# First-stage spectra of a long convolution: stored in 128-row transfers, with 64 low and 26 high frequencies

## Chip, cores and metric

One core of one Trainium2 chip runs the whole program. The metric is the device time of one execution in microseconds (us), as the median of several runs.

## What is computed

A long causal convolution of each of eight sequences with one filter `h`, followed by a mixture of experts with soft slots. Cut to what matters:

```python
# x: (8, 5696, 128), h: (5696, 128)
Xf = rfft(x, n=2*S, axis=1); Hf = rfft(h, n=2*S, axis=0)
y  = irfft(Xf * Hf, n=2*S, axis=1)[:, :S, :]          # (8, 5696, 128)
x  = y.reshape(45568, 128)
logits = x @ phi                                       # 32 slots
d  = softmax over all rows of logits
slot_input = d.T @ x                                   # 32 x 128
slot_out   = relu(slot_input[e] @ w1[e]) @ w2[e]       # 8 experts, 4 slots each
c  = softmax over the slots of logits
out = c @ slot_out                                     # (45568, 128)
```

Everything is float32. The change touches the first stage of the Fourier transform of `h` and of the eight sequences.

## The kernel before

**The transform.** A sequence of 5696 = 89 x 64 positions is read as 89 rows of 64 positions, `n2` = 0..63, each with 128 channels. The first stage (`stage_a`, L230) is a matrix product over the rows that gives 90 frequencies `k1`, with a real and an imaginary part, for every `n2`. The second stage (`stage_b1`, L275) is, for each of the 90 frequencies, a matrix product over the 64 values of `n2`, after which the spectrum is multiplied with that of `h`. `stage_b2` goes back over `n2`, and the stages `c1` to `c6` go back over the rows, form the logits, both softmaxes and the sum over rows. The experts and the output product follow at the end.

**Between the stages the data go through DRAM.** Nine tensors `fd[g]` (g = 0 for `h`, 1 to 8 for the sequences) hold the spectra of the first stage as frequency x `n2` x (real, imaginary) x 128 channels. One value of `n2` is 1 KB, one frequency is a row of 64 KB. `stage_a` writes with short stretches of `n2` for many frequencies; `load_g` (L264) reads 8 frequencies with all 64 `n2` into the tile `gt`, 512 KB at a time, where the 128 partitions are 2 frequencies x 64 `n2`. Likewise `stage_b2` writes its result to the tensors `zm` and `zr`, and `load_main` and `load_rest` read them back into `zc` and `zx`.

**A chunk.** `load_x` brings 89 rows (96 for the sequences, cut at multiples of 16) of 2 x 8 values of `n2`. `fold` (L209, on POOL) adds and subtracts the near and the far positions. A chunk has 4 sums and 4 differences, that is 8 values of `n2`; the sums have the `n2` numbers 0 to 31 and the differences 32 to 63. Eight chunks make one `g`, 72 chunks all of them. The sums (o = 0) and differences (o = 1) go through different columns of the matrix `s1`.

**Low and high.** For each chunk `stage_a(c, False)` computes the low frequencies: two groups (o = 0 and 1) of 64 columns of `s1`, side by side in the 128 output partitions. For each pair of chunks `stage_a(c, True)` computes the high frequencies: four groups (two chunks, o = 0 and 1) of 32 columns. Each call makes two matrix products' worth of PSUM bank (real and imaginary part) and ACT copies both into one tile `fst` of 128 partitions x 4 KB, of which there are four buffers (L233, L243). With LOW = 60, 60 of each 64 low columns and 30 of each 32 high columns hold a frequency.

**Stores.** The stores of `fst` are not issued at once but put on the list `pending` (L221), which `flush` (L223) empties; the line of the issue in the profile is therefore L225. There are two stores of 60 rows for a low tile and four of 30 rows for a high one; a row is 4 KB, 4 values of `n2`. That makes 8 stores for a pair of chunks and 288 in all.

**Order.** The order of the work is written out by hand in the loop over steps `t` from L631. Chunk `t` is computed in step `t`; the second stage follows 9 steps behind (`LAG_B`) with one or two units of 8 frequencies in a step, the back transform 27 steps behind (`LAG_C`). Nearly all DMAs are issued by SP in program order: the loads of `x`, the stores `f<-fst`, the loads `gt<-f` (three buffers, requested three units ahead by `prefetch`, L638), the stores `zm<-zst` and `zr<-zst`, and the loads of `zc` and `zx`. The first load `gt` of a `g` waits until all stores of that `g` have landed. ACT's queue issues only the small constants and eight early stores `zr<-zx` of 24 rows. The very last DMA of the program (L901) writes the last 64 positions of all eight sequences:

```python
nc.sync.dma_start(
    out=ov[:, NV * RW * N2:, :].rearrange("b (j n) d -> b j (n d)", n=CH),
    in_=o_[:, n, :, :].rearrange("p q d -> p (q d)"))
```

Its target runs over 8 sequences and, within each, over 16 rows of 2 KB; its source is one tile of 128 partitions.

Of the kernel before, what the change touches and what calls it, by code (L numbers as in the profile page):

```python
# [11 lines left out]
F32 = mybir.dt.float32  # L12
# [6 lines left out]
def transform_tables(S, N1, N2, CH, LOW, MAIN, XR):  # L19

    N, R1, HALF, P = N1 * N2, S // N2, N2 // 2, 2 * N2
    k1 = np.arange(N1)  # L30
    alpha = np.pi * (k1 + 0.5) / N1
    m1 = np.arange(R1) - (N1 - 1) / 2
    a1 = np.outer(m1, alpha)
    part = np.stack([np.cos(a1), -np.sin(a1), -np.cos(a1)], 1)
    s1 = np.zeros((P, 2, 3, N2 + HALF))
    for i, r in enumerate((slice(0, R1), slice(XR - R1, XR))):
        s1[r, i, :, 0:LOW] = part[:, :, 0:LOW]
        s1[r, i, :, N2:N2 + N1 - LOW] = part[:, :, LOW:]
    a0 = np.outer(alpha, np.arange(N1 // 2) + 0.5)
    part = np.stack([np.cos(a0), -np.sin(a0), -np.cos(a0)], 1)  # L40
    NP = N1 // 2
    im = np.zeros((2, MAIN, 2, N2))
    ir = np.zeros((2, 2, HALF, N2))
    for o in range(2):
        for c in range(2):
            im[o, :, c, 0:NP] = part[0:MAIN, o + c]
            ir[o, c, 0:N1 - MAIN, 0:NP] = part[MAIN:, o + c]
    k2 = np.arange(N2)
    omega = np.pi * (k1[:, None] + 2 * N1 * k2[None] + 0.5) / N
    m2 = np.arange(HALF) - (N2 - 1) / 2  # L50
    a2 = m2[None, :, None] * omega[:, None, :]
    w = np.concatenate([np.cos(a2), np.sin(a2)], 1)
    back = np.arange(N2).reshape(2, HALF).T.reshape(-1)
    NU = (NP + 1) // 2
    turn = (N1 - 1) / 2 * alpha[:, None] + (N2 - 1) / 2 * omega
    wq = np.zeros((2, N2, NP, N2))
    vq = np.zeros((2, N2, NU, 2, N2))
    tn = np.zeros((2, N2, 2, (NU + 1) // 2, 2, 2))
    for a in range(2):
        wq[a] = w[a::2].transpose(1, 0, 2)  # L60
        for q in range(NP):
            vq[q % 2, :, q // 2, a] = w[2 * q + a][back].T
            tn[q % 2, :, 0, q // 4, a, q // 2 % 2] = np.cos(turn[2 * q + a]) / N
            tn[q % 2, :, 1, q // 4, a, q // 2 % 2] = np.sin(turn[2 * q + a]) / N
    im, ir, wq, vq, tn = [t.reshape(P, *t.shape[k:]) for t, k in
                          ((im, 2), (ir, 3), (wq, 2), (vq, 2), (tn, 2))]
    return [np.ascontiguousarray(t, dtype=np.float32) for t in (s1, im, ir, wq, vq, tn)]
# [3 lines left out]
def kernel(  # L71
# [24 lines left out]
    nc = tc.nc  # L96
    P = 128
    B, S, D = x.shape
    NSL = moe_phi.shape[1]
    E, _, F = moe_w1.shape  # L100
    SPE = NSL // E
    NFC = F // P
    N1, N2 = 90, 64
    R1, HALF, NP = S // N2, N2 // 2, N1 // 2
    CH = 4
    NJ = HALF // CH
# [5 lines left out]
    HP = P // 2  # L112
    NQ = NJ // 2
    assert S == R1 * N2 and R1 == N1 - 1 and D == P and CH == Q == 4
    LOW, MAIN = 60, HP
    XR = -(-R1 // 16) * 16
    ctx.enter_context(tc.manual_schedule())

# [1 line left out]
        nc.inline_tensor(t, f"tab_{n}").ap()  # L120
        for n, t in zip(("s1", "im", "ir", "w", "v", "turn"),
                        transform_tables(S, N1, N2, CH, LOW, MAIN, XR))]
    fd = [nc.dram_tensor(f"f_{g}", (N1, N2, 2, D), F32, kind="Internal").ap() for g in range(B + 1)]
    zm = [nc.dram_tensor(f"zm_{b}", (2, MAIN, HALF, 2, D), F32, kind="Internal").ap() for b in range(B)]
    zr = [nc.dram_tensor(f"zr_{b}", (2, 2, HALF, HALF, D), F32, kind="Internal").ap() for b in range(2)]
    cd = nc.dram_tensor("c_t", (P, B * NQ, Q, 2, MH), F32, kind="Internal").ap()
# [24 lines left out]
    front = ExitStack()  # L151
# [15 lines left out]
    def bank():  # L167
        rings.append(rings.pop(0))
        return rings[-1].tile([P, 512], F32, name="bank", tag="bank")
# [51 lines left out]
    pending = []  # L221
# [5 lines left out]
    def columns(c, o):  # L227
        return folded[c][:, o, :, :].rearrange("p n d -> p (n d)")

    def stage_a(c, high):  # L230

        g, j = divmod(c, NJ)
        st = apool.tile([P, CH, 2, D], F32, name="fst", tag="fst", bufs=4)  # L233
        if high:
            groups = [(c_, o, HALF, slice(HP, HP + HALF)) for c_ in (c - 1, c) for o in range(2)]
        else:
            groups = [(c, o, HP, slice(0, HP)) for o in range(2)]
        for q in range(2):
            p = bank()
            for i, (c_, o, m, cols) in enumerate(groups):  # L240
                nc.tensor.matmul(p[i * m:(i + 1) * m, :], s1[:, g // B, q + o, cols], columns(c_, o),  # L241
                                 start=True, stop=True)
            nc.scalar.activation(st[:, :, q, :],  # L243
                                 p[:, :].rearrange("p (n d) -> p n d", d=D), AF.Copy)
        k0, k1 = (LOW, N1) if high else (0, LOW)
        for i, (c_, o, m, _) in enumerate(groups):
            n0 = o * HALF + CH * (c_ % NJ)
            pending.append(partial(
                nc.sync.dma_start,
                out=fd[g][k0:k1, n0:n0 + CH, :, :].rearrange("k n c d -> k (n c d)"),  # L250
                in_=st[i * m:i * m + k1 - k0, :, :, :].rearrange("k n c d -> k (n c d)")))
        if high:
            for c_ in (c - 1, c):
                del folded[c_]
# [369 lines left out]
    for i in range(8):  # L624
        nc.scalar.dma_start(
            out=zr[i // 4][i // 2 % 2, i % 2, N1 - MAIN:].rearrange("k (j r) d -> (k j) (r d)", r=2 * CH),
            in_=zring[0][1][0:4 * (HALF - N1 + MAIN), :, :, :].rearrange("p h n d -> p (h n d)"))
# [3 lines left out]
    for t in range(last_front + 1):  # L631
# [24 lines left out]
        if t < NA:  # L656
            stage_a(t, False)
            fold(t + 1)
# [16 lines left out]
        if t % 2:  # L675
# [10 lines left out]
            if t < NA:  # L686
                stage_a(t, True)
# [54 lines left out]
    for q in range(Q):  # L742
        r = slice(q * NSL, (q + 1) * NSL)
        nc.gpsimd.tensor_copy(out=rep4[r, :, :],
                              in_=ident[r, r].unsqueeze(1).broadcast_to([NSL, Q, NSL]))
# [17 lines left out]
    for V in range(T, NT):  # L763
# [30 lines left out]
        else:  # L794
            for i in range(4 * (V - T - 1), min(4 * (V - T), E), 2):
                nc.sync.dma_start(
                    out=w2s[:, i:i + 2, :, :],
                    in_=moe_w2[i:i + 2].rearrange("e (p c) d -> p e c d", p=P))
# [6 lines left out]
    p = bank()  # L805
# [8 lines left out]
    p = bank()  # L814
# [5 lines left out]
                  ap=[own.ap[0], [NSL + SPE, E], [1, SPE]])  # L820
# [6 lines left out]
    for g in range(EG):  # L827
        for f0 in range(0, F, FH):
            p = bank()
# [3 lines left out]
            dst = hid[:, g, :, f0 // NFC:(f0 + FH) // NFC]  # L833
# [6 lines left out]
    for g in range(EG):  # L840
        for k0 in range(0, NFC, 4):
            p = bank()
            for k in range(4):
# [3 lines left out]
                out=hidT[:, g, k0:k0 + 4, :], in_=p[:, :].rearrange("p (k c) -> p k c", k=4))  # L847
# [9 lines left out]
    p = bank()  # L857
# [18 lines left out]
    for b in range(B):  # L876
        for w0 in range(0, NV, G4):
            n = min(G4, NV - w0)
# [10 lines left out]
            for q in range(Q):  # L889
                dst = o_[:, 0:n + lone, q, :]  # L890
# [7 lines left out]
                out=ov[b, t0:t0 + n * RW * N2, :].rearrange("(w p n) d -> p w (n d)", p=P, n=CH),  # L898
                in_=o_[:, 0:n, :, :].rearrange("p w q d -> p w (q d)"))
            if lone:  # L900
# [3 lines that stand above are left out]
# [29 lines left out]
```

## Time and profile before

| | |
|---|---|
| runs (us) | 909.78, 910.25, 915.08; median 910.25 |
| the profiled execution (us) | 909.23 |
| its span on the core (us) | 907.4 |
| PE busy | 760.2 us (84%) |
| DVE, ACT, POOL busy | 66%, 48%, 44% |
| bytes by DMA | 278.33 MB: HBM read 147.94 MB, written 129.00 MB |
| stores `f<-fst` | 144 of 240 KB and 144 of 120 KB, issued from 15.2 to 656.2 us |
| loads `gt<-f` | 99 of 512 KB and 9 of 128 KB, issued from 49.2 to 720.0 us |

A span is the time from the first to the last instruction of the profiled execution. "Busy" is the time in which an engine executes instructions; the DMA share is the mean busy share of the 16 DMA engines that move the data of all queues. A DMA is cut into packets; for the transfers named here a packet is one contiguous piece of a row. The end of a transfer is marked by packets of 4 bytes, which the counts below include. The column of the granted clock tells which part of TensorE's full clock it was allowed.

### The profile page before, as it was taken

Reading aid. Unit: us, or ns where it says so; the run is one execution under the profiler, and the core shown is the slowest. Engines: PE = TensorE matmul, PEld = TensorE weight load, DVE = VectorE, ACT = ScalarE, POOL = GpSimd, SP = SyncE. Lnnn points to the kernel's source line nnn. Section 1 sums busy time; section 2 is a strip of 40 time slices with the busy share of each in tenths; the row PEclk is TensorE's granted clock in tenths of the full one; section 3 lists DMA queues with packets and bytes.
Section 4 is the critical chain, followed back from the end, with each engine's and each line's share of the span. In section 5 each row is a group of like instructions: output and inputs, shape, how many; then the busy total and the mean of one; then the engine's idle time right before and its main releaser. Section 6 shows DMA issues by size and latency. Waiting matters only on the chain.

```text
span 907.4 us, 21291 instructions
## 1 busy us (share of the span) xinstructions
PE 760.2 (84%) x8308; PEld 387.7 (43%) x8308; DVE 601.4 (66%) x896; ACT 436.8 (48%) x880; POOL 399.8 (44%) x353
## 2 busy tenths in 40 slices
PE   6857778689999989999998999799888877767893
PEld 2212233234444444444444444344444434344793
DVE  2029767568778867886877787678778766653552
ACT  2423234335556545665655655456544444563441
POOL 4634322444555655655655566456332224651000
PEclk9979889999999999999999999899988888766855
DMA  8989999999999999999999999999998768540798
GB/s 267 318 275 343 293 296 337 298 314 376 341 291 375 361 326 308 372 358 299 357 364 335 295 373 348 303 308 346 306 291 304 264 200 341 186 166 1 292 406 335
DMA packets 170443, 278.33 MB, mean 307 GB/s; under 512 B 13543, under 2 KB 128231, under 8 KB 165135
## 3 DMA queue, kind: packets, MB, share of 16 engines
q1 hardware_dynamic: 169336, 275.74, 89.7%
q10 hardware_dynamic: 1008, 1.25, 0.5%
q8 instruction: 66, 1.08, 0.5%
q14 instruction: 33, 0.27, 0.1%
HBM read 147.94 MB, written 129.00 MB: 305 GB/s over the span
## 4 chain that ended last, share of the span: by engine, by line
PE 47%; DMA 23%; ACT 8%; POOL 8%; DVE 6%; issue 6%; SPq 1%; ACTq 0%; DVEq 0%; POOLq 0%
PE bank L241 9%; DMA gt<-f 9%; PE bt L284 9%; PE bz L327 6%; POOL y L430 5%; PE bank L412 4%; DMA f<-fst 4%; PE op L886 3%; PE bank L439 3%; PE bank L417 3%; PE bank L448 2%; DMA zx<-zr 2%; ACT fst L243 2%; DMA out_dram<-o 2%; PE bank L527 2%
## 5 line engine op out<-in xcount | busy, mean ns | idle before, releaser
L241 PE MATMUL bank<-x,s 128*32 128x512 f32 (+1 forms) x1152 | 218.0, 620 | 12.9 <-POOL x L217 8.4
L217 POOL TENSOR_TENSOR x<-xc 128x512 f32<-128x512 f32 x144 | 180.4, 1278 | 107.2 <-PE bank L241 86.5
L284 PE MATMUL bt<-gt,wt 64*64 64x256 f32 x1620 | 125.0, 419 | 72.8 <-DMA gt<-f 33.0
L430 POOL TENSOR_TENSOR y<-y,op 128x512 f32<-128x512 f32 x64 | 77.6, 1213 | 206.8 <-DVE op L404 204.3
L304 DVE TENSOR_TENSOR pi<-bt,Hi 128x1024 f32<-128x1024 f32 x96 | 113.0, 1177 | 83.5 <-PE bt L284 83.3
L243 ACT ACTIVATE fst<-bank 128x512 f32<-128x512 f32 x216 | 122.8, 592 | 86.0 <-PE bank L241 57.7
L332 ACT ACTIVATE zst<-bz 128x1024 f32<-128x1024 f32 x96 | 93.3, 972 | 128.3 <-PE bz L327 109.4
L284 PEld LDWEIGHTS bt<-gt,wt 64*64 64x64 f32 x1620 | 58.3, 141 | 151.2 <-issue 79.1
L312 DVE TENSOR_TENSOR yf<-bt,pi 128x512 f32<-128x512 f32 x192 | 119.4, 663 | 3.3
L304 DVE TENSOR_TENSOR bt<-bt,Hr 128x1024 f32<-128x1024 f32 x96 | 113.0, 1177 | 0.0
L241 PEld LDWEIGHTS bank<-x,s 128*32 128x32 f32 (+1 forms) x1152 | 55.1, 126 | 129.8 <-issue 93.6
L327 PE MATMUL bz<-yf,vt 64*64 64x256 f32 x1440 | 110.4, 404 | 0.0
L327 PEld LDWEIGHTS bz<-yf,vt 64*64 64x64 f32 x1440 | 64.3, 143 | 25.5 <-issue 4.2
L512 POOL TENSOR_TENSOR L<-L,rs 128x512 f32<-128x512 f32 x32 | 33.5, 1048 | 91.6 <-DVE rs L511 66.4
L404 DVE TENSOR_TENSOR y<-bank,y 128x512 f32<-128x512 f32 x32 | 22.1, 692 | 76.7 <-ACT y L420 76.5
L439 PE MATMUL bank<-ident,y 109*128 109x109 f32 x512 | 62.7, 273 | 7.9 <-ACT yt L441 7.9
L504 ACT ACTIVATE L<-L 128x512 f32<-128x512 f32 x32 | 20.2, 630 | 94.7 <-POOL L L501 94.6
L430 POOL TENSOR_TENSOR y<-y,om 128x512 f32<-128x512 f32 x54 | 63.9, 1183 | 2.1
L439 PEld LDWEIGHTS bank<-ident,y 109*128 109x128 f32 x512 | 52.9, 149 | 19.4 <-POOL x L217 14.7
L412 PE MATMUL bank<-zc,im 64*64 64x512 f32 x480 | 60.8, 623 | 0.0
L441 ACT ACTIVATE yt<-bank 128x360 f32<-128x360 f32 x128 | 53.0, 482 | 7.7 <-PE bank L439 7.3
L420 ACT ACTIVATE y<-bank 128x512 f32<-128x512 f32 x32 | 19.1, 596 | 72.6 <-PE bank L417 72.6
(101 smaller groups left out, 862.5 us busy)
## 6 DMA issues: line engine op xcount, KB each, us to landing
gt<-f SPq DMA_DIRECT2D x99, 512.0 KB
f<-fst SPq DMA_DIRECT2D x144, 240.0 KB
zm<-zst SPq DMA_DIRECT2D x128, 256.0 KB
zc<-zm SPq DMA_DIRECT2D x30, 1024.0 KB
xc<-in_x_dram SPq DMA_DIRECT2D x32, 768.0 KB
f<-fst SPq DMA_DIRECT2D x144, 120.0 KB
out_dram<-o SPq DMA_DIRECT2D x16, 1024.0 KB
zx<-zr SPq DMA_DIRECT2D x30, 512.0 KB
```

The source lines that it names most:

```text
L217: nc.gpsimd.tensor_tensor(out=y_[:, o, :, :], in0=near, in1=far, op=AL.subtract if o else AL.add)
L241: nc.tensor.matmul(p[i * m:(i + 1) * m, :], s1[:, g // B, q + o, cols], columns(c_, o), start=True, stop=True)
L243: nc.scalar.activation(st[:, :, q, :], p[:, :].rearrange("p (n d) -> p n d", d=D), AF.Copy)
L284: nc.tensor.matmul(bt[q * HP:(q + 1) * HP, a, o, :], wt[r, 2 * i + q, :], t_[r, 2 * o + q, :, :].rearrange("p c d -> p (c d)"), start=True ...
L304: nc.vector.tensor_tensor(out=p_, in0=pv, in1=h_, op=AL.mult)
L312: nc.vector.tensor_tensor(out=y_[r, 0:k, c, :], in0=pv[:, :, c, :], in1=pi[r, 0:k, 1 - c, :], op=op_)
L327: nc.tensor.matmul(bz[a * HP:(a + 1) * HP, q, o, :], vt[r, i, a, :], y_[r, a * m + o, :, :].rearrange("p c d -> p (c d)"), start=True, sto ...
L332: nc.scalar.activation(st[:, 0:m, 0:n, :].rearrange("p o q x -> p q o x"), bz[:, 0:n, 0:m, :], AF.Copy)
L412: nc.tensor.matmul(ps[o, c][h_ * HP:(h_ + 1) * HP, :], im[r, c, :], zt[r, h_, :, c, :], start=True, stop=False)
L430: eng.tensor_tensor(out=part_, in0=part(v, 0), in1=o_[:, :, :], op=sign)
L439: nc.tensor.transpose(p[:, i * TR:(i + 1) * TR], ys[T][0:TR, k * CH + i, 0:D], ident[0:TR, 0:TR])
L441: nc.scalar.activation(yt[:, k * CH:(k + 1) * CH, :, :], of_tokens(p), AF.Copy)
```

## The change

`LOW` becomes 64, so the low tile holds 64 frequencies in 64 columns and the high tile the other 26 in 32 columns, six of which are empty. `fd[g]` grows to 96 frequency rows, so that the empty ones are stored too. In `fd[g]` the 64 values of `n2` stand in the order of the chunks: chunk, then sums and differences, then the 4 values, and the rows of the matrix `wt` of the second stage are permuted in the same way (`front`). The parts of one `fst` tile then lie next to each other in DRAM, and one store per tile, written with an access pattern made by hand, takes the place of two or four.

```diff
+    front = np.arange(N2).reshape(2, HALF // CH, CH).transpose(1, 0, 2).reshape(-1)
...
-        wq[a] = w[a::2].transpose(1, 0, 2)
+        wq[a] = w[a::2].transpose(1, 0, 2)[front]
...
-    LOW, MAIN = 60, HP
+    LOW, MAIN = HP, HP
...
-    fd = [nc.dram_tensor(f"f_{g}", (N1, N2, 2, D), F32, kind="Internal").ap() for g in range(B + 1)]
+    fd = [nc.dram_tensor(f"f_{g}", (LOW + HALF, N2, 2, D), F32, kind="Internal").ap() for g in range(B + 1)]
...
-        k0, k1 = (LOW, N1) if high else (0, LOW)
-        for i, (c_, o, m, _) in enumerate(groups):
-            n0 = o * HALF + CH * (c_ % NJ)
-            pending.append(partial(
-                nc.sync.dma_start,
-                out=fd[g][k0:k1, n0:n0 + CH, :, :].rearrange("k n c d -> k (n c d)"),
-                in_=st[i * m:i * m + k1 - k0, :, :, :].rearrange("k n c d -> k (n c d)")))
+        k0, m = (LOW, HALF) if high else (0, LOW)
+        j0 = j - high
+        v = fd[g][k0, 2 * CH * j0]
+        dst = [[CH * 2 * D, P // m], [N2 * 2 * D, m], [1, CH * 2 * D]]
+        pending.append(partial(
+            nc.sync.dma_start,
+            out=bass.AP(tensor=v.tensor, offset=v.offset, ap=dst),
+            in_=st[:, :, :, :].rearrange("p n c d -> p (n c d)")))
```

`dst` lists the steps and counts of the target from the outermost on: for a low tile 2 pieces (sums, differences) x 64 frequencies x 1024 elements, for a high tile 4 pieces x 32 frequencies x 1024 elements.

## The prediction

> **What bounds the kernel now.** I first read the page's rows by slice and by queue, then the busy time by stretch, and last single DMAs in the early and the final microseconds.
>
> The page: the slices of the DMA share and rate, the packet total, the queues (packets, MB, share), and the chain of waits by engine.
>
> ```profile
> DMA  8989999999999999999999999999998768540798
> GB/s 267 318 275 343 293 296 337 298 314 376 341 291 375 361 326 308 372 358 299 357 364 335 295 373 348 303 308 346 306 291 304 264 200 341 186 166 1 292 406 335
> DMA packets 170443, 278.33 MB, mean 307 GB/s; under 512 B 13543, under 2 KB 128231, under 8 KB 165135
> ...
> q1 hardware_dynamic: 169336, 275.74, 89.7%
> q10 hardware_dynamic: 1008, 1.25, 0.5%
> ...
> PE 47%; DMA 23%; ACT 8%; POOL 8%; DVE 6%; issue 6%; SPq 1%; ACTq 0%; DVEq 0%; POOLq 0%
> ```
>
> The chain names PE most often, but the DMA engines are at nine tenths or more through three quarters of the span. By stretch (busy us per engine, granted clock, DMA share, GB/s); the first row is the stretch in which `f` is stored, the second the rest:
>
> ```profile
> 15.00:656.00 641.00, 563.71 (x6039) 257.95 (x6039) 450.18 (x643) 324.24 (x626) 326.52 (x275) 0.96 0.99 330
> 656.00:907.00 251.00, 189.82 (x2256) 126.84 (x2255) 145.61 (x246) 110.40 (x252) 67.28 (x67) 0.75 0.71 254
> ```
>
> So for 641 us all 16 engines are full (0.99) at 330 GB/s, which is 330 / 16 / 0.99 = 20.8 GB/s for an engine on this mix of 4 KB, 1 KB and 512 B packets, while PE has 12% to spare. Whatever puts more work on any one engine lengthens this stretch, because the loads that the second stage needs use all of them.
>
> What one engine does alone is seen in the last 13 us, forty slices from 895 to 908 us, where the final stores (2 KB packets) drain:
>
> ```profile
> DMA  9999999999999999999999988721110000000000
> GB/s 410 403 416 416 410 410 403 403 410 410 410 403 416 416 403 410 403 410 410 403 410 397 353 334 334 290 107 57 50 38 25 25 25 6 0 0 0 0 0 25
> ```
>
> 410 / 16 = 25.6 GB/s for an engine, and one engine remains at the end, at 25. A 4 KB packet then takes 0.160 us; the trace's 24,260 packets of 4 KB have a median of 0.159.
>
> **Into how many parts a DMA is split.** This decides the change, and the packet counts tell it. Each engine that takes part ends with a 4-byte packet. Of the 13543 packets under 512 B, 384 are data (`phi`, `turn`, `ir`: 3 x 128 rows of 128, 384 and 256 B), so 13159 are ends. The program has 542 DMAs whose outermost count is a multiple of 16, 288 stores of 60 or 30 rows, 8 stores of 24 rows, 7 loads of 9 rows, and the last store (L901), 8 x 16 rows in DRAM from 128 partitions. 542 x 16 + 288 x 15 + 8 x 12 + 7 x 9 + 1 x 8 = 13159, to the packet: the parts are the largest number up to 16 that divides the outermost counts of both sides. ACT's queue confirms it alone: 832 rows + 5 x 16 + 8 x 12 = 1008. The last store is the row nearest to the change: 128 partitions, but an outermost count of 8 in DRAM, and 8 parts; its tail above is one engine working off its 16 rows in turn.
>
> The new stores have 128 partitions against an outermost count of 2 (low) or 4 (high). By these rows they go to 2 and 4 engines.
>
> Are these always the same engines? Packets carry no engine number, but in two stretches where PE and loads are quiet and only the 15-part stores of `f` are in flight, the share says so:
>
> ```profile
> 22.50:24.00 1.50, 1.08 (x12) 0.13 (x4) 0.00 (x0) 0.00 (x0) 0.00 (x0) 1.00 0.94 229
> 24.00:25.50 1.50, 0.00 (x0) 0.00 (x0) 0.00 (x0) 0.00 (x0) 0.00 (x0) 1.00 0.93 314
> ```
>
> 15 / 16 = 0.94: with several such stores queued, one engine stays idle, so each leaves out the same one. I take the set as fixed, the low stores on engines A and B, the high ones on A to D.
>
> [...]
>
> **The change, part by part.**
>
> *Stores, on the path.* A pair of chunks has two low tiles and one high one. Engine A gets 2 x 64 + 32 = 160 rows of 4 KB, where before each of 15 engines got 4 x 4 + 4 x 2 = 24. In 36 pairs that is 5760 rows or 23.6 MB; at 25.6 GB/s 922 us, at 20.8 GB/s 1134 us. I take 922: the mixed rate has the small packets of other transfers in it.
>
> *Everything else in the stretch.* 330 GB/s x 641 us is 211 MB; without the 53.1 MB of `f` stores (144 x 240 KB + 144 x 120 KB) 158 MB remain, in 16 parts nearly throughout, 9.9 MB for each engine: 475 us at 20.8 GB/s, 387 at 25.6. I take 475, the rate of this very mix.
>
> *Sum.* Engine A needs 922 + 475 = 1397 us for what now takes 641. Can it starve? SP issues in order and stops at waits, but three loads `gt` and up to four `fst` tiles are outstanding, and of a pair's 38.8 us on A (1397 / 36) about two thirds are queued behind the load that PE waits for, against 10 to 15 us from a landing through `stage_b1` to SP's next issue. So A stays busy, and PE, ACT and POOL wait for it. The other 268 us (909.23, the profiled execution's time, less 641) stay: **268 + 1397 = 1665 us**. The profiled time is 1 us under the median, which changes nothing. Bounds: 33.5 MB at 25.6 GB/s gives 1309 + 268 = 1577; at 20.8 GB/s 1611 + 268 = 1879.
>
> *Issues, off the path.* 288 issues of 0.407 us become 108:
>
> ```profile
> L225 SPq DMA_DIRECT2D f<-fst x288: 314/407/1777, 15.2 to 656.2; - x144
> L225 SPq DMA_DIRECT2D zm<-zst x128: 579/609/1847, 115.3 to 722.5; - x128
> ...
> L901 SPq DMA_DIRECT2D out_dram<-o x1: 1030/1030/1030, 895.5 to 895.5; - x1
> ```
>
> The new form is not in the profile; between the nearest rows, 0.609 and 1.030 us, it costs 66 to 111 us against 117. SP saves 6 to 51 us, which count for nothing beside engine A (SPq has 1% of the chain).
>
> *Free.* The matrix products already have 64 and 32 columns, so PE's and ACT's work for empty columns does not change. The empty rows add 3.5 MB, which are in the 160 rows. `load_g` reads the same 1 KB pieces of the same rows; the permutation lies in a constant.
>
> *A new wait.* An `fst` buffer comes free only when its store has landed, behind everything queued on A. ACT waits for that at L243; queued behind it are its copies `zst`, `yt` and `lt`, for which PE and SP wait. This is how the queue on A reaches the other engines, not a cost beside it.
>
> **Rivals.**
>
> *The store is spread by its 128 partitions over 16 engines.* Then each engine has 3 x 8 = 24 rows a pair, as 15 of them have now, and 2592 fewer ends of 9 ns (288 x 15 against 108 x 16), 1.5 us for each engine. At most the 4% (36 us) that the chain gives to `f<-fst` could go: 873 to 909, taken 907, as the full engines are the nearer row. It decides from 14 parts on: 384 rows x 36 x 0.160 us = 2212 us over k parts is less than the 641 - 475 = 166 us at hand only for k above 13. For it: nothing in the counts. Against: 13159, where 16 parts for L901 would have made 13167. 8%.
>
> *Few parts, but on engines that change from store to store.* No engine is overloaded; the extra bytes cost 11 us (3.5 MB at 330 GB/s), and each 10.2 us of a low store (64 x 0.160) on two engines delays the loads behind it by nothing up to the whole, 36 times: 920 to 1290, taken 1000, as most loads are asked for a pair ahead. Against: the 0.94 and 0.93. 4%.
>
> *The high stores miss engines A and B.* A then carries 36 x 128 rows, 737 us: 268 + 737 + 475 = 1480. 4%.
>
> **How the numbers follow.** The forecast has 84%. Its bounds of 1577 and 1879 hold most of it; I open the lower one to 1550 for a tail that gains from TensorE's clock (0.75 there now, after a stretch at 0.96 that becomes half idle), which leaves some 2 in 10 outside with the rivals. A measurement tells about 1% (9 us) from no change: faster 0.04 and same 0.04 are the first rival; slower has the rest.
>
> **What would show it.** If right: 166168 packets on q1 (4320 ends become 72 x 2 + 36 x 4 = 288, 12960 rows become 13824), 9511 under 512 B; in the stretch with stores a DMA share near 0.44 (two engines full, two at 0.47, twelve at 0.34) and some 154 GB/s; PE's busy time as before, at about 46% of the span; waits for `gt<-f` and `f<-fst` at the head of the list. With 167608 packets on q1 the stores were in 16 parts and I am wrong from the start. With 166168 and a time well under 1550 the set of engines is not fixed; over 1880, rows on one engine are dearer than 0.195 us (4 KB at 20.8 GB/s), or A starves.

## The result and the profile after

The changed kernel takes 1601.37 us (median of 4 runs, 1597.76 to 1603.6) against 910.01 us for the kernel before on the same chip: 1.76 times as long, ratio 1.7575 with a 95% interval of 1.7501 to 1.765. The profiled execution took 1602.05 us, its span 1600.3 us.

The page of the changed kernel: DMA share and rate in forty slices, packets, the main queue, and the chain of waits by engine and by line.

```profile
DMA  6224333443555455546554555555555555966459
GB/s 197 82 89 134 119 113 122 164 156 126 176 178 179 159 181 182 183 162 186 175 180 166 176 179 180 171 173 181 182 171 167 175 175 188 308 226 239 157 226 360
DMA packets 167273, 281.84 MB, mean 176 GB/s; under 512 B 9511, under 2 KB 124199, under 8 KB 161967
...
q1 hardware_dynamic: 166168, 279.26, 52.0%
...
DMA 71%; PE 14%; SPq 5%; DVE 3%; issue 2%; ACT 2%; POOL 1%; ACTq 0%; DVEq 0%; POOLq 0%
DMA gt<-f 38%; DMA zc<-zm 15%; DMA f<-fst 11%; DMA zr<-zst 4%; SPq L226 4%; PE bt L286 3%; PE bank L242 3%; DMA zx<-zr 3%; PE bz L329 2%; DMA out_dram<-o 2%; PE op L888 1%; PE bank L414 1%; SPq L272 1%; PE bank L441 1%; PE bank L529 1%
```

The 16 DMA engines were full while `f` was stored (share 0.99) and are now half idle there on average (0.49), yet the chain has gone from PE (47% before) to DMA (71%). Both are true at once because the work is spread unevenly. The packet counts, 166168 and 9511, are those that the prediction gave for stores in 2 and 4 parts.

By stretch (busy us per engine, granted clock, DMA share, GB/s): ten microseconds early on, the stretch in which `f` is stored, and the rest.

```profile
70.00:80.00 10.00, 5.20 (x24) 1.28 (x24) 0.00 (x0) 2.17 (x4) 0.19 (x1) 0.66 0.13 53
15.00:1350.00 1335.00, 691.18 (x6100) 308.53 (x6100) 454.40 (x654) 333.08 (x635) 326.32 (x276) 0.74 0.49 161
1350.00:1600.00 250.00, 186.32 (x2199) 124.35 (x2192) 141.21 (x234) 106.77 (x244) 66.23 (x66) 0.73 0.70 252
```

From 70 to 80 us a low store runs and nothing else: 0.13 x 16 is two engines, 53 GB/s. The whole loss lies in the second row: 1335 us in place of 641, while the rest takes 250 in place of 251. Through that stretch the packet records show fewer than two packets in flight in 0.2% of the time, and exactly two in 29%: that fits engines A and B at work all the time, often alone.

SP's issues from 60 to 125 us, before the second stage begins (start, length, line):

```profile
59.64 4.69 SPq L199 DMA_DIRECT2D xc<-in_x_dram  x1
64.43 21.85 SPq L226 DMA_DIRECT2D f<-fst  x3
86.37 4.69 SPq L199 DMA_DIRECT2D xc<-in_x_dram  x1
91.15 21.86 SPq L226 DMA_DIRECT2D f<-fst  x3
```

The period is 26.72 us per pair of chunks (64.43 to 91.15). In it engine A has 160 rows of 4 KB for the stores and 12 for the load of `x` (96 rows of two pieces over 16 engines): 0.155 us a row. Three issues take 21.85 us, where the median of one was 0.407 us before: SP is held while it issues; that the full engines hold it, until they take more, is the author's guess. Everything behind in SP's order, the loads `gt`, `zc` and `zx` among it, then comes late. The list of waits of the changed kernel (who waited for what: us, times, longest):

```profile
PE bt L286 <- DMA gt<-f: 434.0, 38, 41.1
...
PE bank L414 <- DMA zc<-zm: 103.9, 24, 7.6
...
ACT fst L244 <- DMA f<-fst: 86.8, 10, 15.9
```

PE's wait for `gt` in the kernel before was 33.0 us:

```profile
PE bt L284 <- DMA gt<-f: 33.0, 10, 10.2
```

### The profile page after: what moved, and what is told of

It is laid out like the page before. It is cut to its first block, busy times and chain, and to the rows that moved or that the text cites. A ratio compares the mean times of both kernels' runs of the same rounds, so it can differ in the third digit from the quotient of the medians.

```text
span 1600.3 us, 21033 instructions
## 1 busy us (share of the span) xinstructions
PE 884.1 (55%) x8308; PEld 435.6 (27%) x8308; DVE 601.2 (38%) x896; ACT 441.6 (28%) x880; POOL 398.5 (25%) x353
## 2 busy tenths in 40 slices
DMA packets 167273, 281.84 MB, mean 176 GB/s; under 512 B 9511, under 2 KB 124199, under 8 KB 161967
## 3 DMA queue, kind: packets, MB, share of 16 engines
q1 hardware_dynamic: 166168, 279.26, 52.0%
## 4 chain that ended last, share of the span: by engine, by line
DMA 71%; PE 14%; SPq 5%; DVE 3%; issue 2%; ACT 2%; POOL 1%; ACTq 0%; DVEq 0%; POOLq 0%
DMA gt<-f 38%; DMA zc<-zm 15%; DMA f<-fst 11%; DMA zr<-zst 4%; SPq L226 4%; PE bt L286 3%; PE bank L242 3%; DMA zx<-zr 3%; PE bz L329 2%; DMA out_dram<-o 2%; PE op L888 1%; PE bank L414 1%; SPq L272 1%; PE bank L441 1%; PE bank L529 1%
## 5 line engine op out<-in xcount | busy, mean ns | idle before, releaser
L286 PE MATMUL bt<-gt,wt 64*64 64x256 f32 x1620 | 159.6, 518 | 455.3 <-DMA gt<-f 434.0
L242 PE MATMUL bank<-x,s 128*32 128x512 f32 (+1 forms) x1152 | 234.3, 665 | 63.1 <-ACT fst L244 54.7
L286 PEld LDWEIGHTS bt<-gt,wt 64*64 64x64 f32 x1620 | 72.2, 173 | 552.7 <-issue 489.5
L414 PE MATMUL bank<-zc,im 64*64 64x512 f32 x480 | 93.4, 890 | 103.9 <-DMA zc<-zm 103.9
L329 PE MATMUL bz<-yf,vt 64*64 64x256 f32 x1440 | 133.7, 473 | 0.0
L306 DVE TENSOR_TENSOR pi<-bt,turn 128x1024 f32<-128x1024 f32 (+1 forms) x12 | 14.1, 1176 | 200.0 <-PE bt L286 200.0
L329 PEld LDWEIGHTS bz<-yf,vt 64*64 64x64 f32 x1440 | 76.8, 171 | 36.6 <-issue 18.2
L414 PEld LDWEIGHTS bank<-zc,im 64*64 64x64 f32 x480 | 31.4, 185 | 150.3 <-issue 132.9
L419 PE MATMUL bank<-zx,ir 26*64 26x512 f32 x480 | 44.6, 810 | 42.3 <-DMA zx<-zr 42.3
```

The lines of the kernel that those rows point to most:

```text
L286: nc.tensor.matmul(bt[q * HP:(q + 1) * HP, a, o, :], wt[r, 2 * i + q, :], t_[r, 2 * o + q, :, :].rearrange("p c d -> p (c d)"), start=True ...
L306: nc.vector.tensor_tensor(out=p_, in0=pv, in1=h_, op=AL.mult)
L329: nc.tensor.matmul(bz[a * HP:(a + 1) * HP, q, o, :], vt[r, i, a, :], y_[r, a * m + o, :, :].rearrange("p c d -> p (c d)"), start=True, sto ...
L414: nc.tensor.matmul(ps[o, c][h_ * HP:(h_ + 1) * HP, :], im[r, c, :], zt[r, h_, :, c, :], start=True, stop=False)
```

## The experiments

The theory: a store is worked off by as many engines as divide the outermost counts of both its sides (up to 16), always by the same ones, and engine A's rows set the time. A result without an interval is a single execution.

**Stores taken apart, the rest of the change kept.**

```diff
...
-            out=bass.AP(tensor=v.tensor, offset=v.offset, ap=dst),
-            in_=st[:, :, :, :].rearrange("p n c d -> p (n c d)")))
+        for i in range(P // m):
+            n0 = CH * (2 * j0 + i)
+            rows = m
...
+                out=fd[g][k0:k0 + rows, n0:n0 + CH, :, :].rearrange("k n c d -> k (n c d)"),
+                in_=st[i * m:i * m + rows, :, :, :].rearrange("k n c d -> k (n c d)")))
```

> Layout, order of n2, 64 and 26 frequencies and empty rows as in the changed kernel; only the one store per tile is taken apart again into two of 64 rows or four of 32. Theory (a store is worked by as many engines as divide both outermost counts, always the same ones): 16 parts each, 24 rows of 4 KB per engine and pair as before the change, so 905 to 925 us, the extra 3.5 MB included. Rival (the new layout, the empty rows or the 96-row tensor cost the time): near 1600 us.

Measured 928.41 us (922.49 to 931.51), ratio 1.0177 (1.0137 to 1.0216). Its stretch from 15 to 656 us:

```profile
15.00:656.00 641.00, 559.10 (x5901) 254.95 (x5900) 440.36 (x630) 318.32 (x613) 319.92 (x270) 0.95 0.99 328
```

All engines are full again. With the layout, the empty rows and the 96-row tensor kept, the kernel is 1.8% slower than before, not 76%; the form of the store has the rest. The last 3 us over the expected range are followed up below.

**Only the low, or only the high stores whole.** The same edit, for high tiles alone and for low tiles alone.

> The changed kernel with the low stores whole (2 parts) and the high ones taken apart into four of 32 rows (16 parts). Theory, with the high stores of the changed kernel on engines that include A and B: rows on A per pair 128 + 8 = 136, 136 x 36 x 0.160 = 783 us, and 412 + 268 us of the changed kernel's run for the rest: 1463 us. Rival (the four engines of the high stores are others): no gain from this, near 1600 us.

> The changed kernel with the high stores whole (4 parts) and the low ones taken apart into two of 64 rows (16 parts). Theory: rows on A per pair 32 + 16 = 48, 276 us, and 412 to 475 + 268 us for the rest: 956 to 1019 us. Rival (a 128-row store with a hand-made pattern is slow whatever its parts): a third of such stores is left, so about a third of the 692 us, 1140 us.

Measured 1481.59 and 1032.15 us. Taking the high stores off engine A gains 120 us, so their four engines include A; and a third of the stores whole costs 120 us over the kernel before (912.18 us in these runs), not a third of 692. The first came 19 us over the theory's number, the second 13 us over the upper end of its range, which the table below takes up.

**The old kernel with one number changed.**

```diff
-    LOW, MAIN = 60, HP
+    LOW, MAIN = 62, HP
```

> The kernel before the change with one number changed: 62 low and 28 high frequencies instead of 60 and 30. Nothing of the change is in it: the stores are single pieces, 62 rows and 28 rows, in the old layout. Theory: 62 rows go to 2 engines (31 each), 28 rows to 14 (2 each): 4 x 31 + 4 x 2 = 132 rows on A per pair, 760 us, + 412 + 268 = 1440 us. Rival (the hand-made pattern, the layout or the size of the new stores is the cause): 910 us as before.

Measured 1469.98 us. Nothing of the change is in this kernel, and it loses 558 us against the kernel before (912.18 us) for two frequencies more in the low tile; the theory's number was 30 us lower. Its main queue:

```profile
q1 hardware_dynamic: 167320, 275.73, 57.8%
```

169336 before, less 288 x 15 ends, plus 144 x 2 + 144 x 14, is 167320. The rival falls: neither the hand-made pattern nor the layout nor the size of the stores is needed.

**61 and 29, both prime.**

```diff
-    LOW, MAIN = 60, HP
+    LOW, MAIN = 61, HP
```

> The kernel before the change with 61 low and 29 high frequencies, both prime: by the theory every store has one part, all on engine A: 4 x 61 + 4 x 29 = 360 rows per pair, 12960 in all. At the 0.160 us a row of the prediction 2074 + 412 + 268 = 2754 us; at the 0.139 us a row by which the changed kernel and the run with whole low stores differ (120.5 us for 864 rows) 1602 + 7200 x 0.139 = 2603 us. Rival (the count of rows must be even or near a power of two, or a store cannot fall under 2 engines): 1440 to 1600 us.

Measured 2675.53 us, nearly three times the time before. The rate from 60 to 90 us of this run, in forty slices, beside the DMA share of the same slices:

```profile
DMA  0000000000939930000000000000000000000000
GB/s 22 27 27 27 27 27 22 27 27 27 180 131 366 268 93 27 27 22 27 27 27 27 22 27 27 27 27 27 33 16 27 27 27 27 27 22 27 27 27 27
```

One engine, at 27 GB/s or a little less, and a burst where a load of `h` uses all. While one store works alone, its rows start 155 ns apart in the median. In the packet records exactly one packet is in flight in 68% of the stretch with stores (15 to 2420 us). So a store does fall to a single engine, and 288 stores in a row to the same one. 2675.53 lies between the two sizes that were expected.

**Another queue.** The stores of the changed kernel issued by ACT, then by POOL.

```diff
-            nc.sync.dma_start,
+            nc.scalar.dma_start,
```

> The changed kernel, its 108 stores of f issued by ACT in place of SP: another queue, but by the theory the same engines A to D. Theory (engine A's work is the bound, not the order in SP's queue): 5760 rows stay on A, 1560 to 1650 us, or somewhat more where ACT's copies wait behind its issues. Rival (the loads only wait because they stand behind the stores in SP's queue): they pass, 950 to 1200 us.

Measured 1592.48 us, within 1% of the changed kernel. PE's wait for `gt` shrinks from 434.0 to 231.2 us with the stores out of SP's order, but PE now waits for ACT's copies, which stand behind ACT's issues (17.3 us for the same line in the changed kernel):

```profile
PE bt L286 <- DMA gt<-f: 231.2, 29, 29.9
PE bank L493 <- ACT dt L484: 214.8, 32, 15.6
```

The time alone could thus be a wait that has moved. The packet records settle it: from 16 to 1340 us two packets or more are in flight in 99.6% of the time, against 99.8% in the changed kernel. The rows on engines A and B bind, not the order in SP's queue. These records also show the set of engines: ACT's queue carries almost nothing but the stores, and no more than four of its packets of 4 KB are in flight in 99.6% of the time. The two engines of the low stores are thus among the four of the high ones.

```diff
-            nc.sync.dma_start,
+            nc.gpsimd.dma_start,
```

> The changed kernel, its 108 stores of f issued by POOL in place of SP, nothing else. [...] If the low number of parts is itself the cost, or POOL's stores also stay on the same engines: 1550 to 1650 us.

Measured 1180.5 us: most of the loss goes. The time is far under 1550 us, and 80 us over the 920 to 1100 us that the author estimated for stores whose engines change; it lies in the 920 to 1290 us of the prediction's second rival. The stores now have a queue of another kind (its line among the queues, and the landing times of `f<-fst`):

```profile
q0 software_dynamic: 93888, 56.94, 18.8%
```

```profile
DMA to landing us min/median/max: 12.3/18.7/24.6
```

By the packet records 13824 of the 93888 packets are the rows, whole, with 4096 bytes each; the other 80064 have 4 bytes. Stores on 2 and 4 engines fit this to the packet, if each store has 16 ends and an engine without rows gets a 4-byte packet for every row of an engine with rows: 72 x (14 x 64 + 16) + 36 x (12 x 32 + 16) = 80064. Whether the engines change is seen in the rows in flight. On ACT's queue, with four fixed engines, no more than four were in flight in 99.6% of the time; here it is five or more in 31% of the time from 16 to 920 us, six in 88% of the time from 48 to 50 us and eight in 78% of the time from 60 to 62 us. So by this fit a store still goes to two or four engines, but different stores go to different ones. The low number of parts alone therefore does not cost the 692 us; that they are always the same engines costs the larger part, 421 us (1602.05 to 1180.5). Why the time stays above 1100 us is open.

**Three buffers for the stored tile.**

```diff
-        st = apool.tile([P, CH, 2, D], F32, name="fst", tag="fst", bufs=4)
+        st = apool.tile([P, CH, 2, D], F32, name="fst", tag="fst", bufs=3)
```

> The changed kernel with three buffers for the tile that is stored, in place of four. Theory (engine A always has work queued, so its 5760 rows set the time): 1590 to 1640 us. Rival (the time is the latency of a store against the four buffers it is turned around in): a quarter fewer buffers lengthen the stretch with stores well beyond that, over 1700 us.

Measured 1602.07 us. ACT waits 389.1 us for `f<-fst` to land in place of 86.8, and the time stays: the turnaround of the buffers is not the limit.

**What the 1.8% is.** In all of the following kernels every store has 13 to 16 parts. First, the stores taken apart, without the empty rows in the high ones:

```diff
-            rows = m
+            rows = N1 - LOW if high else m
```

> As the run with all stores taken apart (two of 64, four per high tile), but the high stores leave out the six empty rows: 26 rows each, 13 parts of 2 rows. The run with 32 rows was 1.8% slower than the kernel before. If the 3.5 MB of empty rows cost that (11 us at 330 GB/s): 908 to 916 us. If the order of n2 in DRAM or the 64-row stores cost it: it stays at 920 to 930 us.

Measured 930.14 us, 1.0188 (1.0150 to 1.0227): the empty rows are not it. Then the kernel before with `LOW` = 64 alone, and the kernel before with the new order of `n2` alone:

```diff
-    LOW, MAIN = 60, HP
+    LOW, MAIN = HP, HP
```

```diff
+    front = np.arange(N2).reshape(2, HALF // CH, CH).transpose(1, 0, 2).reshape(-1)
...
-        wq[a] = w[a::2].transpose(1, 0, 2)
+        wq[a] = w[a::2].transpose(1, 0, 2)[front]
...
-            n0 = o * HALF + CH * (c_ % NJ)
+            n0 = CH * (2 * (c_ % NJ) + o)
```

> The kernel before with 64 low and 26 high frequencies, old order of n2 and old layout: stores of 64 rows (16 parts of 4) and of 26 rows (13 parts of 2). What costs the two runs with stores taken apart 1.8%? If the 64-row stores do (their issue is longer than that of 60 rows on SP, and no engine is left free): 925 to 932 us here. If the order of n2 in DRAM does: 908 to 915 us.

> The kernel before with 60 and 30 frequencies as they were, and only n2 in the order of the chunks in DRAM, the rows of wt permuted to match. If the order costs the 1.8%: 925 to 932 us here. If the 64-row stores do: 908 to 915 us.

Measured 923.4 us, 1.0124 (1.0078 to 1.0169), just under its range, and 914.78 us, 1.0009 (0.9979 to 1.0040). The order costs nothing that these runs can tell; the stores of 64 and 26 rows cost most of it. Last, an attempt to beat both kernels (the load of `gt` is changed to read the same padded rows):

```diff
-    fd = [nc.dram_tensor(f"f_{g}", (N1, N2, 2, D), F32, kind="Internal").ap() for g in range(B + 1)]
+    fd = [nc.dram_tensor(f"f_{g}", (N1 // 2, 2 * N2 + CH, 2, D), F32, kind="Internal").ap() for g in range(B + 1)]
...
-                out=fd[g][k0:k1, n0:n0 + CH, :, :].rearrange("k n c d -> k (n c d)"),
+                out=bass.AP(tensor=fd[g].tensor, offset=fd[g][k0 // 2, n0].offset,
+                            ap=[[(2 * N2 + CH) * 2 * D, (k1 - k0) // 2], [N2 * 2 * D, 2], [1, CH * 2 * D]]),
...
```

> The kernel before with 4 KB of padding after every second frequency in DRAM, so that the rows of a store are 64 and 68 KB apart in turn. In the profile before, where stores of 60 and 30 rows were alone on the engines from 22.5 to 24 us, they ran at 229 GB/s, against 410 at the end of the program. [...]

Measured 930.48 us, 1.0191 (1.0155 to 1.0226). The padding was tried in case the pitch of exactly 64 KB makes the 4 KB packets of the kernel before as long as they are in the mean, 195.0 ns against a median of 159. The author's estimate from these was a gain of up to 36 ns x 12960 / 16 = 29 us, 880 to 905 us in all, and 905 to 930 us without it. The gain did not come, and the packets did not get shorter: 201.5 ns in the mean. That the pitch of 64 KB costs time is not shown. The issues of the stores (min, median, max in ns), first with 64 frequencies in the low tile, then with the padding:

```profile
L225 SPq DMA_DIRECT2D f<-fst x288: 297/489/1828, 15.3 to 679.1; - x144
```

```profile
L225 SPq DMA_DIRECT2D f<-fst x288: 797/827/2348, 15.6 to 677.9; - x144
```

Both issue longer than the 407 ns of the kernel before, and both are 1 to 2% slower; but the loss does not grow with the issue time (489 ns and 1.2%, 827 ns and 1.9%), so that the issues are the cause is a guess. In both traces all packets together also take longer, 836 us for each engine against 823 before and 829 with the new order alone; why is open. No version tried beats the kernel before.

## Why the prediction was right

Engine A's rows against time, for the runs whose stores bind on A. "Rest" is the time less 268 us, the part outside the stretch, and less the rows at 0.155 us.

| kernel | parts low, high | rows on A | us | rest, us |
|---|---|---|---|---|
| high stores whole | 16, 4 | 1728 | 1032.15 | 496 |
| 62 and 28 frequencies | 2, 14 | 4752 | 1469.98 | 465 |
| low stores whole | 2, 16 | 4896 | 1481.59 | 455 |
| the changed kernel (profiled) | 2, 4 | 5760 | 1602.05 | 441 |
| 61 and 29 frequencies | 1, 1 | 12960 | 2675.53 | 399 |

- **What bounds it before, and the parts.** Right. The rule read from the 13159 ends gave the packets of every later run whose stores stay on SP's and ACT's queues: 166168 for the change, 167320 and 165304 for 62 and 61 frequencies, 168328 for each half of the change.
- **The same engines each time.** Right: a single engine at 27 GB/s through 288 stores, and 120 us for the high stores' share of A. No more than four rows of the stores in flight on ACT's queue, and up to eight on POOL's, where the engines change, confirm it. The prediction had only the 0.94 and 0.93 of two stretches of 1.5 us for this, thin evidence that held.
- **The first term, 922 us.** The mechanism is right, the size 29 us too large: the row's price came from 2 KB packets (25.6 GB/s, 0.160 us); rows of 4 KB start 0.155 us apart, so 893 us.
- **The second term, 475 us.** Too large as well: 1335 - 893 leaves 442. It was priced at 20.8 GB/s, the rate of 16 full engines. The table shows the rest falling as A's rows grow, from 496 to 399 us for the same 9.9 MB. That A moves its share faster because the other engines are mostly idle by then fits the falling DMA share of the stretch (0.87, 0.49 and 0.27 in the first, fourth and fifth row), but no run takes this by itself. The two terms together make the 62 us by which 1397 missed 1335; the sum of 1665 missed 1602 by 63. Both erred to the same side, so the hit is not two errors that cancel.
- **A does not starve.** Right: fewer than two packets are in flight in 0.2% of the stretch, and three buffers in place of four change nothing. The picture of what is queued was incomplete. SP itself is held at the issue of a store, which the prediction did not see. Its estimate of 0.609 to 1.030 us for an issue holds for the median (0.632) and not for the longest (10.419), but as the run on ACT's queue shows, SP's time was not the bound.
- **The tail.** Its 268 us became 267. The lower end of the range was opened for a higher TensorE clock there; the clock was 0.73 in place of 0.75 (0.74 with 61 frequencies), so a gain from an idler stretch ahead of the tail is not shown.
- **The share of 0.44, 154 GB/s, and PE's busy time.** The share came out at 0.49 with 161 GB/s. PE's busy time was expected unchanged and rose from 760.2 to 884.1 us, which cost nothing here and is taken up below.
- **The rivals.** Spreading by the 128 partitions and moving engines are refuted by the counts and by the single engine; on POOL's queue, where the engines do move, the time is 1180.5 us. High stores that miss A and B are refuted by the run with the low stores whole.

## What to carry to other kernels

Before merging DMAs, write down the outermost count of both sides: their largest common divisor up to 16 is the number of engines, by every packet count here on SP's and ACT's queues (13159 ends before, 166168 packets after), and a transfer that looks better by size can run on two engines of 16 (53 GB/s here). Transfers with few parts from one of these queues also fell on the same engines again and again: one engine at 27 GB/s for the stores of one part, and no more than four rows in flight in 99.6% of the time on ACT's queue. Where the engines are full, work out the bytes of the busiest one engine, not the mean; a mean share of 0.49 was a full stop here. The profile of the old kernel could tell it: its count of 4-byte ends is the sum of the parts of all transfers and so tests a rule for them, and a form like the new one (here the very last store) may already be in it.

## What was not expected of the hardware

In these runs PE's clock is lower where PE waits more. The mean granted clock was 0.903 before, 0.861 with the high stores whole, 0.764 with 62 frequencies, 0.739 in the changed kernel and 0.640 with 61 frequencies, with 33.0, 123.7, 321.7, 434.0 and 1140.9 us of PE's wait for `gt`; in ten microseconds of that last run without a matmul it stood at 0.50.

```profile
70.00:80.00 10.00, 0.00 (x0) 0.00 (x0) 0.00 (x0) 0.00 (x0) 0.00 (x0) 0.50 0.12 40
```

The matmuls of the second stage (64x256) took 518 ns in the mean in the changed kernel, 419 before, in the same shape:

```profile
L284 PE MATMUL bt<-gt,wt 64*64 64x256 f32 x1620 | 125.0, 419 | 72.8 <-DMA gt<-f 33.0
```

```profile
L286 PE MATMUL bt<-gt,wt 64*64 64x256 f32 x1620 | 159.6, 518 | 455.3 <-DMA gt<-f 434.0
```

That is 1.24 times as long, at a clock lower by a factor of 1.22 (0.903 / 0.739). These kernels, which wait for their DMAs, thus show a PE that is both idler and slower: 884.1 us busy in place of 760.2, for 8308 matmuls in both, must not be read as more work.

A form of store also changes what SP pays to issue it: 0.407 us in the median for rows of 60 and 30, 0.827 for the same rows in blocks of two.
